# Score banks in a pool of their own, output sums in four one-bank tiles, and one store for each last result

## The chip, the cores and the metric

The kernel runs on one NeuronCore of a Trainium2 chip. The metric is device time in microseconds (us) for one launch. TensorE (PE in the profile) multiplies matrices; VectorE (DVE) and ScalarE (ACT) do elementwise work and are the only engines here that read PSUM, the accumulators' memory of eight banks of 128 x 512 float32; GpSimd (POOL) helps with splits of operands; SyncE (SP) issues nearly all DMAs. An engine runs its instructions in the order in which they were written for it, and waits on semaphores for the others.

## The reference

Attention with a threshold, then two MLPs in a row over the same 2304 tokens. All is float32.

```
scores = (q @ k^T) / 8                      # 4 batches, 8 heads, 576 x 576, head size 64
scores = where(scores >= max(scores) - tau, scores, -1e9)
attn   = softmax(scores);  y = attn @ v
x  = y, heads laid side by side              # 2304 x 512
h  = x @ w_in;   g = max(h, 0) + alpha * min(h, 0);   x = g @ w_out      # 512 -> 2048 -> 512
h  = x @ w2_in;  g = h - tanh(h);                     out = g @ w2_out   # 512 -> 2048 -> 512
```

## The kernel before

The tokens are cut into nine blocks of 256. Float32 operands are split into a high and a low part, and each product is three matmuls (high x high, low x high, high x low). Attention, the first MLP (blocks m = 0 to 8) and the second (m = 9 to 17) overlap. Each MLP block has eight pairs of steps over the 2048 hidden columns: `h_pair` or `twin_pair` computes h in the tiles `hp`, `pt` or `acc` (L915, L869), `split` makes g and its parts, `acc_pair` multiplies by the output weights and sums over the pairs.

All instructions are recorded with estimated costs and ranks, ordered once by the planner `Plan.order`, and then written out in that order with `run()`. The planner knows banks by keys of its own (`("c", 0)` to `("c", 3)` for the four output banks). The waits on semaphores are laid later, by the tile framework, and it keeps its books by tile: whoever touches a tile that another engine wrote or read waits for it, whichever columns it was.

PSUM is shared out at the start (L273 to L276). `sc` is two tiles of 1024 columns, so two banks each; `acc` two tiles of one bank; `hp` and `pt` one bank each. In attention a tile of `sc` holds the 576 scores of one head. Later its four banks hold output sums:

- In the last two blocks of the first MLP, which run as one ("wide"), `wide_products` (L1104) sums four column groups c = 0 to 3 into `acc[0]`, `acc[1]` and the two banks of `sc[1]`. At the end ScalarE copies c = 2, 3, 0, 1 out (`drain`, L1114), each is stored to DRAM and read back for the second MLP.
- In the second MLP `out_products` runs. Six of the eight pairs use Strassen's seven products (`emit_seven`, L1032) and two use plain ones (`emit_plain`, L1039). The quarter sums lie in half banks: numbers 1 and 6 in bank 0, 2 and 3 in bank 1, 7 and 5 in bank 2, 4 and 8 in bank 3. Banks 0 and 1 are the tile `sc[0]`, banks 2 and 3 `sc[1]`. A plain pair adds only to banks 1 and 3.
- After the eighth pair of a block ScalarE copies number 1 out of bank 0 (`p1`, L1062), VectorE adds numbers 6, 7, 5 and 5 to it in four operations of 128 x 256 (L1065), and then adds the whole banks 1 and 3 in two operations of 128 x 512 (`both`). Each of these two is followed by its store (`store`).

Rows of `out` go by batch, 576 each. Blocks 9 to 16 store 128 neighbouring rows with one DMA (L1085). Block 17 holds the last 64 rows of each of four batches, so its two results are stored as two pieces of 64 rows each (L1089), four DMAs in all.

Of the kernel before, what the change touches and what calls it, by code (L numbers as in the profile page):

```python
# [24 lines left out]
P = 128  # L25
# [53 lines left out]
class Plan:  # L79
# [9 lines left out]
    def add(self, engines, rank, emit, reads=(), writes=(), banks=(), takes=(), lag=0.0, after=(), late=False):  # L89

        n = len(self.ops)
        deps, order = set(), set(after)
        for k in reads:
            deps.update(self.written.get(k, ()))
        for k in writes:
            deps.update(self.written.get(k, ()))  # L100
            deps.update(self.read.get(k, ()))
        for k in reads:
            self.read.setdefault(k, []).append(n)
        for k in writes:
            self.written[k] = [n]
            self.read[k] = []
        for k in {k[:2] for k in (*reads, *writes)}:
            self.users.setdefault(k, []).append(n)
        for tag, _ in takes:
            if tag != "rw":  # L110
                if self.takers.get(tag, n) != n:
                    order.add(self.takers[tag])
                self.takers[tag] = n
        deps.discard(n)
        self.ops.append((engines, rank, emit, deps, order - deps, banks, takes, lag, "DVE" in engines and not banks and engines["DVE"] > 0.1, late))
        return n
# [119 lines left out]
def attention_mlp_mlp(ctx: ExitStack, tc: tile.TileContext, kv, q0, q1, tau, w1i, w1o, alpha, w2i, w2o, out):  # L236
# [33 lines left out]

    sc = [ppool.tile([P, 1024], F32, name=f"sc{k}") for k in range(2)]  # L273
    acc = [ppool.tile([P, 512], F32, name=f"acc{t}") for t in range(2)]
    hp = ppool.tile([P, 2, BLK], F32, name="hp")
    pt = ppool.tile([P, 4, P], F32, name="pt")  # L276

    hps = hp, pt.rearrange("p (k c) s -> p k (c s)", k=2)

# [9 lines left out]
    def take(pool, key, shape, dtype, tag, bufs):  # L289
        T[key] = pool.tile(shape, dtype, tag=tag, name=tag, bufs=bufs)  # L290
        return T[key]
# [716 lines left out]

    def half_bank(n):
        k = {1: 0, 6: 1, 2: 2, 3: 3, 7: 4, 5: 5, 4: 6, 8: 7}[n]  # L1010
        return sc[k // 4][:, k % 4 * BLK:(k % 4 + 1) * BLK], k // 2

    def two_banks(k):
        return sc[k // 2][:, k % 2 * 512:(k % 2 + 1) * 512]

    def out_products(p, rank):
        m, n = p // NPAIR, p % NPAIR
        w, g = ("wp", n), ("g", p)
        strassen = n in STRASSEN
        begins = n == out_order(m)[0]  # L1020

        seven = [(0, 0, 1), (2, 1, 2), (1, 6, 4), (3, 3, 5), (4, 4, 6), (5, 5, 7), (6, 2, 3)]
        begun_banks = set()

        def emit_seven(e, now):
            gh, gl = T[g], T["gl", p]
            wh, wl = T[w]
            for a, b, number in now:
                a, b = slice(a * P, (a + 1) * P), slice(b * BLK, (b + 1) * BLK)
                out_, bank = half_bank(number)  # L1030
                for i, (x, y) in enumerate(((gl, wh), (gh, wh), (gh, wl))):
                    e.matmul(out_, lhsT=x[:, a], rhs=y[:, b], start=(begins and i == 0 and number in (1, 2, 5, 4)),  # L1032
                             stop=(n == NPAIR - 1 and i == 2), skip_group_check=True)

        def emit_plain(e, k, t):
            wh, wl = (x[:, k * 512:(k + 1) * 512] for x in T[w])
            gh, gl = (T[g][:, part, k, t * P:(t + 1) * P] for part in range(2))
            for i, (x, y) in enumerate(((gl, wh), (gh, wh), (gh, wl))):
                e.matmul(two_banks(3 - 2 * t), lhsT=x, rhs=y, start=False, stop=(n == NPAIR - 1 and k == 1 and i == 2), skip_group_check=True)  # L1039

        if strassen:
            rows = [(*w, k, part) for k in range(4) for part in range(2)]
            for k, now in enumerate((seven[:1], seven[1:3], seven[3:5], seven[5:])):
                halves = {half_bank(x[2])[1] for x in now}
                add({"PE": 0.36 * len(now)}, rank + MLP_PE, lambda e, now=now: emit_seven(e, now), [*rows, (*g, 0), (*g, 1), ("gl", p, 0), ("gl", p, 1)],
                    [("c", x) for x in halves], [("c", x) for x in halves])
        else:
            for t in (1, 0):
                for k in range(2):
                    x = 3 - 2 * t  # L1050
                    add({"PE": 0.69}, rank + MLP_PE, lambda e, k=k, t=t: emit_plain(e, k, t), [(*w, k, 0), (*w, k, 1), (*g, 0), (*g, 1)], [("c", x)], [("c", x)])
        if n < NPAIR - 1:
            return
        o = [("o", 2 * m + t) for t in range(2)]

        def bank(number):
            return half_bank(number)[0]

        def p1(e):
            for k in range(2):  # L1060
                take(apool, o[k], [P, 512], F32, "o", BUFS["o"])
            copy(e, T[o[1]][:, :BLK], bank(1))  # L1062

        def total(e, out_, x, y):
            e.tensor_tensor(out=out_, in0=x, in1=y, op=ALU.add)  # L1065

        r = rank + MLP_G
        a, b = (lambda: T[o[1]][:, :BLK]), (lambda: T[o[1]][:, BLK:])
        c, d = (lambda: T[o[0]][:, :BLK]), (lambda: T[o[0]][:, BLK:])
        oa, ob, oc, od = [(*o[1], 0)], [(*o[1], 1)], [(*o[0], 0)], [(*o[0], 1)]  # L1070
        add({"ACT": 0.3}, r, p1, [("c", 0)], oa + [o[0], o[1]], [("c", 0)], takes=[("o", x) for x in o])
        add({"DVE": 0.35}, r, lambda e: total(e, b(), bank(6), a()), [("c", 0), *oa], ob, [("c", 0)])
        add({"DVE": 0.35}, r, lambda e: total(e, c(), bank(7), b()), [("c", 2), *ob], oc, [("c", 2)])
        add({"DVE": 0.35}, r, lambda e: total(e, d(), bank(5), c()), [("c", 2), *oc], od, [("c", 2)])
        add({"DVE": 0.35}, r, lambda e: total(e, b(), bank(5), b()), [("c", 2), *oc], ob, [("c", 2)])
        for t in (1, 0):
            x = 3 - 2 * t

            def both(e, t=t, x=x):
                total(e, T[o[t]], two_banks(x), T[o[t]])  # L1080

            def store(e, t=t):
                if m < 2 * NBLK - 1:
                    row = (m - NBLK) // 2 * S + (m - NBLK) % 2 * BLK + t * P
                    e.dma_start(out=out[row:row + P, :], in_=T[o[t]])  # L1085
                else:
                    for k in range(2):
                        row = (2 * t + k + 1) * S - D
                        e.dma_start(out=out[row:row + D, :], in_=T[o[t]][k * D:(k + 1) * D, :])  # L1089

            z = oa + ob if t else oc + od
            add({"DVE": 0.6}, r, both, [("c", x), *z], z, [("c", x)])
            add({"SYNC": 1.2}, r, store, z, [("out", m, t)], lag=3.0)

    def wide_products(p, rank):
        f = p - (NBLK - 2) * NPAIR
        banks = [acc[0], acc[1], two_banks(2), two_banks(3)]
        keys = [("acc", 0), ("acc", 1), ("c", 2), ("c", 3)]
        for c in range(4):
            def emit(e, c=c):  # L1100
                gh, gl = (T["g", p][:, part] for part in range(2))
                hi, lo = (weight(0, "o", part, f // 4)[:, f % 4, c * P:(c + 1) * P] for part in range(2))
                for n, (w, g) in enumerate(((hi, gh), (hi, gl), (lo, gh))):
                    e.matmul(banks[c], lhsT=w, rhs=g, start=(f == 0 and n == 0), stop=(f == NF - 1 and n == 2))  # L1104

            reads = [("w", (0, "o", f // 4), f % 4, part) for part in range(2)]
            add({"PE": 0.69}, rank + MLP_PE, emit, [*reads, ("g", p, 0), ("g", p, 1)], [keys[c]], [keys[c]])
        if f < NF - 1:
            return
        for c in (2, 3, 0, 1):  # L1110
            o = ("o", 2 * (NBLK - 2) + c)

            def drain(e, c=c, o=o):
                copy(e, take(apool, o, [P, 512], F32, "o", BUFS["o"]), banks[c])  # L1114

            def store(e, c=c, o=o):
                e.dma_start(out=wide_x1d[:, c], in_=T[o].rearrange("p (m s) -> p m s", m=2))

            add({"ACT": 0.478}, rank + MLP_G, drain, [keys[c]], [o], [keys[c]], takes=[("o", o)])
            add({"SYNC": 1.2}, rank + MLP_G, store, [o], [("x1d", m, c) for m in (NBLK - 2, NBLK - 1)], lag=3.0)  # L1120
# [199 lines left out]
```

## Time and profile before

| | us |
|---|---|
| median of 3 runs | 1054.56 (1054.54 to 1054.87) |
| the profiled execution: its time | 1052.59 |
| the profiled execution: its span in the trace | 1050.8 |
| TensorE busy (PE) | 1023.7 |
| VectorE busy (DVE) | 772.9 |
| ScalarE busy (ACT) | 618.4 |

The span is what the trace covers; the time of the same execution is 1.79 us longer, and the median of the runs another 1.97 us. Times in rows are from the start of the span. An end of a busy stretch of PE is modelled, and matmuls that follow one another overlap in the rows: a row of "x12" starts with its first matmul and ends with its last.

### The profile page before, as it was taken

To read this page: it belongs to the slowest core of one execution; us is meant where nothing else is said; L and a number is where in the kernel's file an instruction comes from. 1 tells how busy PE (TensorE), PEld (TensorE's weight loads), DVE (VectorE), ACT (ScalarE), POOL (GpSimd) and SP (SyncE) were. 2 spreads that over 40 slices of the span, in tenths; PEclk is the share of its full clock that TensorE was granted. 3 is DMA by queue.
4 is the path that set the end of the run, shared out by engine and by line. 5 is a ranking of instruction groups with operands and counts; after the bars stand their busy time and mean duration, and the time that the engine had idled before them with its cause. 6 is when DMAs were issued, how large, how long until landed. Compare 5 with 4: busy or idle time off the path is not lost.

```text
span 1050.8 us, 22486 instructions
## 1 busy us (share of the span) xinstructions
PE 1023.7 (97%) x8859; PEld 928.2 (88%) x8859; DVE 772.9 (74%) x1738; ACT 618.4 (59%) x1287; POOL 74.4 (7%) x101
## 2 busy tenths in 40 slices
PE   9979989999999999999999999999999999999997
PEld 7769879999999999998999888998898898899886
DVE  6998989878788778887857787674584484485465
ACT  6988888788788788887846554442312222331321
POOL 0122121001110111101100000000000000000000
PEclk9999999999999999999999999999999999999999
DMA  6678988758786557775585433200010010010000
GB/s 195 191 181 190 209 199 176 136 109 160 141 148 136 124 120 150 140 124 119 96 219 180 135 125 116 80 21 1 21 41 21 21 41 21 21 41 21 1 21 21
DMA packets 188890, 110.76 MB, mean 105 GB/s; under 512 B 158688, under 2 KB 171248, under 8 KB 188784
## 3 DMA queue, kind: packets, MB, share of 16 engines
q1 hardware_dynamic: 188480, 108.51, 44.8%
q8 instruction: 69, 1.13, 0.4%
q10 hardware_dynamic: 304, 0.82, 0.3%
q14 instruction: 37, 0.30, 0.1%
HBM read 61.58 MB, written 9.96 MB: 68 GB/s over the span
## 4 chain that ended last, share of the span: by engine, by line
PE 59%; DVE 2%; ACT 1%; DMA 1%; issue 1%; SPq 0%; DVEq 0%; ACTq 0%
PE sc L1032 13%; PE hp L915 10%; PE acc L869 6%; PE pt L915 5%; PE acc L1140 5%; PE sc L1039 5%; PE pt L869 3%; PE hp L869 3%; PE pt L679 2%; PE sc L1104 2%; PE acc L1104 2%; PE sc L700 1%; DVE st L573 1%; DMA eT<-rw 0%; ACT e L300 0%
## 5 line engine op out<-in xcount | busy, mean ns | idle before, releaser
L915 PE MATMUL hp<-x,i 128*128 128x256 f32 (+1 forms) x1584 | 230.9, 291 | 12.8 <-ACT e L300 5.6
L915 PEld LDWEIGHTS hp<-x,i 128*128 128x128 f32 x1584 | 206.1, 191 | 24.5 <-ACT e L300 6.1
L1140 PE MATMUL acc<-g,o 128*128 128x256 f32 x1232 | 165.7, 279 | 0.8 <-POOL g L303 0.8
L1140 PEld LDWEIGHTS acc<-g,o 128*128 128x128 f32 x1232 | 152.6, 188 | 4.4 <-POOL g L303 1.0
L300 ACT ACTIVATE e<-sc,st,qscale 128x576 f32<-128x576 f32 x144 | 118.0, 828 | 31.1 <-DVE st L576 18.9
L1032 PE MATMUL sc<-wp,g 128*128 128x256 f32 x756 | 135.8, 280 | 0.0
L1032 PEld LDWEIGHTS sc<-wp,g 128*128 128x128 f32 x756 | 115.8, 188 | 1.3
L618 DVE SCALAR_TENSOR_TENSOR rw<-e,st,rw 128x576 f16<-128x576 f32 x128 | 104.7, 835 | 10.3 <-ACT rw L295 9.7
L573 DVE TENSOR_REDUCE st<-sc 128x1 f32<-128x576 f32 x144 | 102.6, 750 | 13.1 <-PE sc L700 12.1
L583 ACT ACTIVATE e<-e,natau 128x576 f32<-128x576 f32 x144 | 110.9, 774 | 0.2
L1032 PE MATMUL sc<-wp,rw 128*128 128x256 f32 x378 | 106.1, 281 | 0.8 <-ACT o L295 0.8
L295 ACT ACTIVATE rw<-e,st 128x576 f16<-128x576 f32 x103 | 78.1, 771 | 18.3 <-DVE st L589 8.0
L295 ACT ACTIVATE g<-mr 128x512 fp32r<-128x512 f32 (+1 forms) x99 | 59.1, 597 | 47.8 <-PE sc L1104 16.7
L679 PE MATMUL pt<-eT,vs 128*64 128x256 f16 (+1 forms) x1584 | 73.3, 247 | 0.2 <-DMA eT<-rw 0.2
L1032 PEld LDWEIGHTS sc<-wp,rw 128*128 128x128 f32 x378 | 71.2, 188 | 2.3 <-ACT o L295 1.0
L303 DVE TENSOR_TENSOR g<-mr,g 128x512 fp32r<-128x512 f32 x80 | 55.6, 695 | 18.9 <-ACT g L295 18.4
L679 PEld LDWEIGHTS <-vs 128*64 128x64 bf16 x1584 | 65.0, 111 | 4.8 <-issue 0.4
L700 PE MATMUL sc<-kh,qh 64*128 64x320 f32 (+1 forms) x672 | 61.7, 310 | 4.4 <-ACT e L300 4.3
L869 PE MATMUL acc<-x,i 128*128 128x512 f32 x264 | 65.5, 395 | 0.0
L700 PEld LDWEIGHTS sc<-kh,qh 64*128 64x128 f32 x672 | 49.1, 185 | 13.2 <-ACT e L300 5.5
L869 PEld LDWEIGHTS acc<-x,i 128*128 128x128 f32 x264 | 48.9, 187 | 11.4
L915 PE MATMUL pt<-x,i 128*128 128x256 f32 (+1 forms) x352 | 58.0, 311 | 0.0
(246 smaller groups left out, 1707.4 us busy)
## 6 DMA issues: line engine op xcount, KB each, us to landing
vs<-in_kv_dram SPq DMA_DIRECT2D x58, 160.0 KB, 3.0
rw<-in_w1o_dram SPq DMA_DIRECT2D x16, 512.0 KB, 4.6
rw<-in_w2i_dram SPq DMA_DIRECT2D x16, 512.0 KB, 4.8
rw<-in_w2o_dram SPq DMA_DIRECT2D x16, 512.0 KB, 4.0
rw<-in_kv_dram SPq DMA_DIRECT2D x56, 144.0 KB, 3.0
rw<-in_w1i_dram SPq DMA_DIRECT2D x15, 512.0 KB, 4.8
out_dram<-o SPq DMA_DIRECT2D x16, 256.0 KB, 2.0
x1d<-o SPq DMA_DIRECT2D x14, 256.0 KB, 2.8
```

What stands on the lines that cost most here:

```text
L295: e.activation(out=out_, in_=in_, func=AF.Copy, **({} if scale is None else {"scale": scale}))
L300: e.activation(out=out_, in_=in_, func=AF.Prelu, alpha=alpha, **kw)
L303: e.tensor_tensor(out=out_, in0=in_, in1=hi.bitcast(F32), op=ALU.subtract)
L573: e.tensor_reduce(out=T[st][:, 0, j:j + 1], in_=x(s), axis=AX.X, op=ALU.max, negate=True)
L583: e.activation(out=w_, in_=w_, func=AF.Exp, bias=natau, scale=1.0, accum_out=T[st][:, 2, j:j + 1])
L618: e.scalar_tensor_tensor(out=x_[:, S + D:], in0=w_, scalar=r, in1=x_[:, :S], op0=ALU.mult, op1=ALU.subtract)
L679: e.matmul(po[HALVES[a]], lhsT=plane((k, a), part, c), rhs=eT(a, block), start=(i == 0), stop=(i == len(TERMS) - 1), skip_group_check=True)
L700: e.matmul(to(a, c), lhsT=x[HALVES[a], s], rhs=y[HALVES[a], c], start=(i == 0), stop=(i == len(terms) - 1))
L869: e.matmul(hq[k], lhsT=weight(1, "i", part, f // 4)[:, c, (f % 4) * P:(f % 4 + 1) * P], rhs=slots_of_x[x][:, :, c, :], start=(n0 + i == 0) ...
L915: e.matmul(hq if both_blocks else hq[:, k, :], lhsT=weight(l, "i", part, f // 4)[:, c, (f % 4) * P:(f % 4 + 1) * P], rhs=slots_of_x[x][:, ...
L1032: e.matmul(out_, lhsT=x[:, a], rhs=y[:, b], start=(begins and i == 0 and number in (1, 2, 5, 4)), stop=(n == NPAIR - 1 and i == 2), skip_g ...
L1140: e.matmul(acc[t][:, (c % 2) * BLK:(c % 2 + 1) * BLK], lhsT=w[:, c * P:(c + 1) * P], rhs=g[:, k, :], start=(f == 0 and n == 0 and c % 2 == ...
```

## The change

It does three things. The two `sc` tiles move from the general PSUM pool to a pool of their own, `spool`. That pool is released when the first output product is written out, and a new pool takes its four banks as four tiles `out0` to `out3` of one bank each; `two_banks` and `half_bank` hand these out, and `wide_products` fetches them only when it emits. And the last block stores each of its two results with one DMA, whose DRAM side is two pieces of 64 rows.

```
-    sc = [ppool.tile([P, 1024], F32, name=f"sc{k}") for k in range(2)]
     acc = [ppool.tile([P, 512], F32, name=f"acc{t}") for t in range(2)]
     hp = ppool.tile([P, 2, BLK], F32, name="hp")
     pt = ppool.tile([P, 4, P], F32, name="pt")
+    spool = tc.alloc_tile_pool(name="spool", bufs=1, space=PSUM)
+    sc = [spool.tile([P, 1024], F32, name=f"sc{k}") for k in range(2)]
+    banks_of_out = []
 
     hps = hp, pt.rearrange("p (k c) s -> p k (c s)", k=2)
 
...
 
     def half_bank(n):
         k = {1: 0, 6: 1, 2: 2, 3: 3, 7: 4, 5: 5, 4: 6, 8: 7}[n]
-        return sc[k // 4][:, k % 4 * BLK:(k % 4 + 1) * BLK], k // 2
+        return two_banks(k // 2)[:, k % 2 * BLK:(k % 2 + 1) * BLK], k // 2
 
     def two_banks(k):
-        return sc[k // 2][:, k % 2 * 512:(k % 2 + 1) * 512]
+        if not banks_of_out:
+            spool.release()
+            mpool = ctx.enter_context(tc.tile_pool(name="mpool", bufs=1, space=PSUM))
+            banks_of_out.extend(mpool.tile([P, 512], F32, name=f"out{n}") for n in range(4))
+        return banks_of_out[k]
 
     def out_products(p, rank):
         m, n = p // NPAIR, p % NPAIR
...
                     row = (m - NBLK) // 2 * S + (m - NBLK) % 2 * BLK + t * P
                     e.dma_start(out=out[row:row + P, :], in_=T[o[t]])
                 else:
-                    for k in range(2):
-                        row = (2 * t + k + 1) * S - D
-                        e.dma_start(out=out[row:row + D, :], in_=T[o[t]][k * D:(k + 1) * D, :])
+                    ends = out.rearrange("(b s) d -> b s d", s=S)[2 * t:2 * t + 2, S - D:, :]
+                    e.dma_start(out=ends, in_=T[o[t]])
 
             z = oa + ob if t else oc + od
             add({"DVE": 0.6}, r, both, [("c", x), *z], z, [("c", x)])
-            add({"SYNC": 1.2}, r, store, z, [("out", m, t)], lag=3.0)
+            add({"SYNC": 0.7}, r, store, z, [("out", m, t)], lag=3.0)
 
     def wide_products(p, rank):
         f = p - (NBLK - 2) * NPAIR
-        banks = [acc[0], acc[1], two_banks(2), two_banks(3)]
+        def home_of(c):
+            return acc[c] if c < 2 else two_banks(c)
+
         keys = [("acc", 0), ("acc", 1), ("c", 2), ("c", 3)]
         for c in range(4):
             def emit(e, c=c):
                 gh, gl = (T["g", p][:, part] for part in range(2))
                 hi, lo = (weight(0, "o", part, f // 4)[:, f % 4, c * P:(c + 1) * P] for part in range(2))
                 for n, (w, g) in enumerate(((hi, gh), (hi, gl), (lo, gh))):
-                    e.matmul(banks[c], lhsT=w, rhs=g, start=(f == 0 and n == 0), stop=(f == NF - 1 and n == 2))
+                    e.matmul(home_of(c), lhsT=w, rhs=g, start=(f == 0 and n == 0), stop=(f == NF - 1 and n == 2))
 
             reads = [("w", (0, "o", f // 4), f % 4, part) for part in range(2)]
             add({"PE": 0.69}, rank + MLP_PE, emit, [*reads, ("g", p, 0), ("g", p, 1)], [keys[c]], [keys[c]])
...
             o = ("o", 2 * (NBLK - 2) + c)
 
             def drain(e, c=c, o=o):
-                copy(e, take(apool, o, [P, 512], F32, "o", BUFS["o"]), banks[c])
+                copy(e, take(apool, o, [P, 512], F32, "o", BUFS["o"]), home_of(c))
 
             def store(e, c=c, o=o):
                 e.dma_start(out=wide_x1d[:, c], in_=T[o].rearrange("p (m s) -> p m s", m=2))
```

The order in which instructions stand on each engine does not move, apart from the stores; what moves are names and waits. In the rows below the number behind a tile's name tells tiles of one name apart (`sc0_89` is `sc[0]`, `out1_105` is `out1`), and in brackets stand the semaphores waited for: an engine's own counter, or one of the DMA's (DMAHW). Line numbers after are 2 to 7 higher (L1032 is L1038, L1039 is L1045, L1065 is L1071, L1089 is L1094).

ScalarE, at the end of the first MLP, where it copies out c = 2 and c = 3. Before:

```order
L927 ACTIVATE mr_9950<-pt_94 128x512 [waits DVE_49,PE_49]
L295 ACTIVATE o_9964<-sc1_90 128x512 [waits PE_49]
L295 ACTIVATE o_9972<-sc1_90 128x512
L295 ACTIVATE o_10012<-acc0_91 128x512 [waits DMAHW7_49,Activation_49]
L927 ACTIVATE mr_10024<-hp_93 128x512 [waits DVE_49,PE_49]
```

And in the changed kernel:

```order
L929 ACTIVATE mr_9961<-pt_92 128x512 [waits DVE_49,PE_49]
L297 ACTIVATE o_9975<-out2_106 128x512 [waits PE_49]
L297 ACTIVATE o_9983<-out3_107 128x512 [waits PE_49]
L297 ACTIVATE o_10023<-acc0_89 128x512 [waits DMAHW7_49,Activation_49]
L929 ACTIVATE mr_10035<-hp_91 128x512 [waits DVE_49,PE_49]
```

Before, the first copy waited for the last product of either column group, since both write `sc1`. Now each waits for the last product of its own group. The matmul that follows on TensorE and writes bank 2 waited for both copies; now it waits for the first, and one nine matmuls later, which writes bank 3, for the second.

TensorE, its last plain pair (t = 1 adds to bank 1, t = 0 to bank 3). Before:

```order
L1039 MATMUL sc0_89<-wp0_10255,g_13500 128x512 [waits DVE_49,Activation_49]
L1039 MATMUL sc0_89<-wp0_10255,g_13500 128x512
L1039 MATMUL sc0_89<-wp1_10256,g_13500 128x512
L1039 MATMUL sc0_89<-wp0_10255,g_13500 128x512 [waits DVE_49]
L1039 MATMUL sc0_89<-wp0_10255,g_13500 128x512
L1039 MATMUL sc0_89<-wp1_10256,g_13500 128x512
L1039 MATMUL sc1_90<-wp0_10255,g_13500 128x512 [waits DVE_49]
L1039 MATMUL sc1_90<-wp0_10255,g_13500 128x512
L1039 MATMUL sc1_90<-wp1_10256,g_13500 128x512
L1039 MATMUL sc1_90<-wp0_10255,g_13500 128x512 x2
L1039 MATMUL sc1_90<-wp1_10256,g_13500 128x512
```

And in the changed kernel:

```order
L1045 MATMUL out1_105<-wp0_10266,g_13511 128x512 [waits DVE_49]
L1045 MATMUL out1_105<-wp0_10266,g_13511 128x512
L1045 MATMUL out1_105<-wp1_10267,g_13511 128x512
L1045 MATMUL out1_105<-wp0_10266,g_13511 128x512 x2
L1045 MATMUL out1_105<-wp1_10267,g_13511 128x512
L1045 MATMUL out3_107<-wp0_10266,g_13511 128x512 x2
L1045 MATMUL out3_107<-wp1_10267,g_13511 128x512
L1045 MATMUL out3_107<-wp0_10266,g_13511 128x512 x2
L1045 MATMUL out3_107<-wp1_10267,g_13511 128x512
```

Before, the three waits are for the copy of number 1, the first add and the fourth add, which all read the other bank of the same tile. Now the one wait left is for g, the operand. On the other side ScalarE's copy now waits for the last product into bank 0, VectorE's first add for that copy alone, and its second for the last product into bank 2.

SyncE, the last stores. Before:

```order
L1085 DMA out_0_dram<-o_12743 128x512 [waits DMAHW7_49,DVE_49]
L1085 DMA out_0_dram<-o_13239 128x512 [waits DMAHW0_49,DVE_49,Activation_49]
L1085 DMA out_0_dram<-o_13238 128x512 [waits DMAHW1_49,DVE_49]
L1089 DMA out_0_dram<-o_13522 64x512 [waits DVE_49,Activation_49]
L1089 DMA out_0_dram<-o_13522 64x512 [waits DMAHW3_49]
L1089 DMA out_0_dram<-o_13521 64x512 [waits DMAHW4_49,DVE_49]
L1089 DMA out_0_dram<-o_13521 64x512 [waits DMAHW5_49]
```

And in the changed kernel:

```order
L822 DMA rw_12578<-wide_x1d_79 128x4x256 [waits DMAHW5_49,DMAHW2_49,DVE_49]
L1091 DMA out_0_dram<-o_13250 128x512 [waits DMAHW0_49,DVE_49,Activation_49]
L1091 DMA out_0_dram<-o_13249 128x512 [waits DMAHW1_49,DVE_49]
L1094 DMA out_0_dram<-o_13533 2x64x512 [waits DVE_49,Activation_49]
L1094 DMA out_0_dram<-o_13532 2x64x512 [waits DMAHW3_49,DVE_49]
```

Four stores of 64 rows have become two whose DRAM side counts 2, then 64, then 512; the side in SBUF counts 128 partitions, as in the other stores.

## Rows read from the trace of the kernel before

**Rows 1.** The page's head and the engines' busy time over the span.

```profile
span 1050.8 us, 22486 instructions
...
PE 1023.7 (97%) x8859; PEld 928.2 (88%) x8859; DVE 772.9 (74%) x1738; ACT 618.4 (59%) x1287; POOL 74.4 (7%) x101
```

**Rows 2.** TensorE's waits, 600 to 1051 us: total, times, longest.

```profile
PE sc L1039 <- DVE o L1065: 0.9, 2, 0.6
PE sc L1032 <- ACT o L295: 0.8, 1, 0.8
PE sc L1039 <- ACT o L295: 0.5, 1, 0.5
```

**Rows 3.** Timeline, end of the first MLP: start, duration, work, [idle before].

```profile
661.31 0.39 PE L1104 MATMUL sc<-g,o3b 128*128 128x512 f32 x1
...
662.01 0.40 PE L1104 MATMUL sc<-g,o3b 128*128 128x512 f32 x1
662.25 0.28 PE L1032 MATMUL sc<-wp,rw 128*128 128x256 f32 x1
...
662.44 1.09 ACT L295 ACTIVATE o<-sc 128x512 f32<-128x512 f32 x2 [2.20 <-PE sc L1104]
...
663.58 0.38 PE L1032 MATMUL sc<-wp,rw 128*128 128x256 f32 x1 [0.83 <-ACT o L295]
```

**Rows 4.** Timeline, TensorE going from Strassen to plain products without a wait.

```profile
1030.70 0.40 PE L1032 MATMUL sc<-wp,g 128*128 128x256 f32 x2
...
1030.94 2.92 PE L1039 MATMUL sc<-wp,g 128*128 128x512 f32 x12
```

**Rows 5.** Timeline, the last 11 us.

```profile
1040.18 0.40 PE L1032 MATMUL sc<-wp,g 128*128 128x256 f32 x2
...
1040.88 0.40 PE L1032 MATMUL sc<-wp,g 128*128 128x256 f32 x2
1041.32 0.39 ACT L295 ACTIVATE o<-sc 128x256 f32<-128x256 f32 x1 [4.36 <-PE sc L1032]
...
1042.81 2.47 DVE L1065 TENSOR_TENSOR o<-sc,o 128x256 f32<-128x256 f32 x5 [2.81 <-PE sc L1039]
...
1044.54 1.66 PE L1039 MATMUL sc<-wp,g 128*128 128x512 f32 x6 [0.29 <-DVE o L1065]
1045.35 2.70 SPq L1089 DMA_DIRECT2D out_dram<-o  x4
1046.23 0.69 DVE L1065 TENSOR_TENSOR o<-sc,o 128x512 f32<-128x512 f32 x1 [0.96 <-PE sc L1039]
```

**Rows 6.** Chain of waits, the third and fourth add of the last block.

```profile
1043.72 0.77 DVE o L1065 x2
```

**Rows 7.** Timeline of SyncE's queue, the third and fourth of the last stores.

```profile
1046.95 1.10 SPq L1089 DMA_DIRECT2D out_dram<-o  x2
```

**Rows 8.** Line 1089, stores of 64 rows: ns min/median/max of an issue; landing.

```profile
L1089 SPq DMA_DIRECT2D out_dram<-o x4: 466/565/587, 1045.4 to 1047.5; - x4
...
DMA to landing us min/median/max: 2.2/2.3/2.4
```

**Rows 9.** Line 1085, stores of 128 rows, the same columns.

```profile
L1085 SPq DMA_DIRECT2D out_dram<-o x16: 332/333/348, 702.7 to 1022.2; - x16
...
DMA to landing us min/median/max: 2.0/2.0/4.1
```

**Rows 10.** DMA view, 1045.3 to 1050 us in 40 slices: busy tenths, packets, queue.

```profile
DMA  0000000000469968897983046996779896200000
...
DMA packets 320, 0.52 MB, mean 112 GB/s; under 512 B 64, under 2 KB 64, under 8 KB 320
...
q1 hardware_dynamic: 320, 0.52, 48.2%
```

**Rows 11.** DMA view, 1020.1 to 1024.6 us, two stores of line 1085.

```profile
DMA packets 289, 0.53 MB, mean 118 GB/s; under 512 B 32, under 2 KB 32, under 8 KB 288
...
q1 hardware_dynamic: 288, 0.52, 30.6%
```

More of the change, by code (lines that the diff above doesn't have):

```diff
@@ L276, in attention_mlp_mlp @@
     pt = ppool.tile([P, 4, P], F32, name="pt")
+    spool = tc.alloc_tile_pool(name="spool", bufs=1, space=PSUM)
+    sc = [spool.tile([P, 1024], F32, name=f"sc{k}") for k in range(2)]
+    banks_of_out = []
     hps = hp, pt.rearrange("p (k c) s -> p k (c s)", k=2)
@@ L1010, in half_bank @@
         k = {1: 0, 6: 1, 2: 2, 3: 3, 7: 4, 5: 5, 4: 6, 8: 7}[n]
-        return sc[k // 4][:, k % 4 * BLK:(k % 4 + 1) * BLK], k // 2
+        return two_banks(k // 2)[:, k % 2 * BLK:(k % 2 + 1) * BLK], k // 2
     def two_banks(k):
-        return sc[k // 2][:, k % 2 * 512:(k % 2 + 1) * 512]
+        if not banks_of_out:
+            spool.release()
+            mpool = ctx.enter_context(tc.tile_pool(name="mpool", bufs=1, space=PSUM))
+            banks_of_out.extend(mpool.tile([P, 512], F32, name=f"out{n}") for n in range(4))
+        return banks_of_out[k]
     def out_products(p, rank):
@@ L1086, in store, with home_of @@
                 else:
-                    for k in range(2):
-                        row = (2 * t + k + 1) * S - D
-                        e.dma_start(out=out[row:row + D, :], in_=T[o[t]][k * D:(k + 1) * D, :])
+                    ends = out.rearrange("(b s) d -> b s d", s=S)[2 * t:2 * t + 2, S - D:, :]
+                    e.dma_start(out=ends, in_=T[o[t]])
             z = oa + ob if t else oc + od
             add({"DVE": 0.6}, r, both, [("c", x), *z], z, [("c", x)])
-            add({"SYNC": 1.2}, r, store, z, [("out", m, t)], lag=3.0)
+            add({"SYNC": 0.7}, r, store, z, [("out", m, t)], lag=3.0)
     def wide_products(p, rank):
         f = p - (NBLK - 2) * NPAIR
-        banks = [acc[0], acc[1], two_banks(2), two_banks(3)]
+        def home_of(c):
+            return acc[c] if c < 2 else two_banks(c)
         keys = [("acc", 0), ("acc", 1), ("c", 2), ("c", 3)]
@@ L1103, in emit @@
                 for n, (w, g) in enumerate(((hi, gh), (hi, gl), (lo, gh))):
-                    e.matmul(banks[c], lhsT=w, rhs=g, start=(f == 0 and n == 0), stop=(f == NF - 1 and n == 2))
+                    e.matmul(home_of(c), lhsT=w, rhs=g, start=(f == 0 and n == 0), stop=(f == NF - 1 and n == 2))
             reads = [("w", (0, "o", f // 4), f % 4, part) for part in range(2)]
@@ L1113, in drain @@
             def drain(e, c=c, o=o):
-                copy(e, take(apool, o, [P, 512], F32, "o", BUFS["o"]), banks[c])
+                copy(e, take(apool, o, [P, 512], F32, "o", BUFS["o"]), home_of(c))
             def store(e, c=c, o=o):
```

1 line of the change is left out of this document (removed).

## The prediction

> **What bounds the kernel now.** I read the page's head first: TensorE is busy 1023.7 of 1050.8 us, so other engines matter only where TensorE waits or where nothing follows it [rows 1]. The view of TensorE's waits from 600 us on shows how rare that is: four waits in all, 0.8 us for ScalarE at one place and 0.9 and 0.5 us at another [rows 2]. The timeline puts the first at 663 us, between the two MLPs [rows 3], the other three behind 1041 us, in the last pair [rows 5]. So no wait of TensorE that the change removes in the blocks between is worth anything: there TensorE is never late, and VectorE's and ScalarE's adds lie beside its next block. Worth something are the change of MLPs and the tail, and in the tail also the stores, since nothing lies beside them.
>
> **Between the MLPs.** ScalarE copies out c = 2 and then c = 3 in 1.09 us, from 662.44 on, 0.03 us after the last product of c = 3 (662.01 + 0.40). It had been idle for 2.20 us. TensorE does three matmuls of line 1032 from 662.25 and resumes only at 663.58 [rows 3]. With a tile for each bank the first copy waits for the products of c = 2 alone, which end at 661.31 + 0.39 = 661.70: it runs from 661.73 to about 662.33. TensorE would go on after three matmuls of 0.12 us each (two take from 1030.70 to 1030.94 [rows 4]), at 662.61, and finds bank 2 free. The second copy ends at about 663.0, and bank 3 is wanted nine matmuls later, at 663.69. The gain is 663.58 - 662.61 = 0.97 us. It is kept: what follows is paced by TensorE without a wait up to 1041 us [rows 2], and the work of VectorE, ScalarE and the loads there is set off by it, so it comes earlier too. What is late next is nothing.
>
> **A wait that is added.** The first product into a new tile waits for the last score product, 583 instructions earlier on TensorE itself. It is long done; I cost it at nothing, and were it to drain the array once, it would be one matmul, 0.4 us [rows 3]. Waits that only move, at the beginnings of blocks, are for work that TensorE waited for before too.
>
> **The last pair.** Before, matmuls and adds take turns, since banks 0 and 1 are one tile. TensorE's last Strassen pair of matmuls starts at 1040.88 [rows 5]; without a wait the twelve plain ones start 0.24 us later and take 2.92 us [rows 4]: 1041.12 to 1044.04. They need only g, which was ready before them. Bank 0 has its last product two triples before the end, at 1040.18 + 0.40 = 1040.58. ScalarE's copy then takes 0.39 us, to about 1041.0, and the four adds, which take 1043.72 + 0.77 - 1042.81 = 1.68 us [rows 5, 6], end at 1042.7. The fifth, on bank 1, whose six matmuls end near 1042.7 as well (five steps of 0.23 us, and the last one's 0.39 us), ends 0.79 us later as it did before (1042.81 + 2.47 - 1044.49), at 1043.51 instead of 1045.28. The sixth follows the last matmul, 1044.06 + 0.69 = 1044.75, instead of 1046.92. So the two results are there 1.77 and 2.17 us earlier, and 0.97 us more with the gain above: 1042.54 and 1043.78.
>
> **The stores.** Before, the four issues take 2.70 us from 1045.35; the third starts at 1046.95 and the fourth, 1.10 - 0.57 us later, at 1047.48 [rows 5, 7, 8]. The span ends 3.32 us after that. The strip of DMA activity shows data from slice 10, 1046.48, which is 1.13 us after the first issue, to the end of slice 34, 1049.41, which is 1.39 us before the end of the span [rows 1, 10]. Two of four issues of 0.57 us go. What the new form of store costs no row shows, so I bound it by the number of DMA engines that share it:
>
> - Sixteen. Then it is a store of 128 rows like line 1085's, landing in 2.0 us [rows 9], plus 0.24 us for the slower issue (565 against 332 ns [rows 8, 9]): 2.24 us, against 2.3 before. The span would end 3.26 us after the second issue at 1043.81, at 1047.07: 3.73 us earlier.
> - Two. The DRAM side of the new form counts 2 outermost. If engines are dealt whole outermost pieces, 64 rows fall to each of two engines. A packet of one row, 2048 bytes, holds an engine for 86 ns where 128 partitions are stored (30.6% of 16 engines for 4.5 us, over 256 packets [rows 11]) and 142 ns in the tail, where 64 are (48.2% for 4.7 us [rows 10]). Both stores go the same way, one behind the other: 128 packets x 86 ns = 11.01 us on each of the two. The first is issued 0.07 us after its add, at 1042.61, and data begins 1.13 us later, at 1043.74; the last ends at 1054.75, and 1.39 us more make 1056.14: 5.34 us later than before. At 142 ns it would be 18.2 us, and 12.5 us later; if an engine had two packets in hand at a time, 5.5 us, and 0.2 us earlier than before.
>
> Which one? Every DMA of the kernel before has an outermost count of 16, 64, 128 or 512 on both sides, and the view counts 64 closing packets under 512 bytes for the four stores of the tail and 32 for two stores of line 1085: sixteen each [rows 10, 11]. That fits dealing by outermost pieces, and it would fit dealing by single rows. But the first explains sixteen closings for all these lists from one number of each list, and a list that counts 2 is the first that has fewer pieces than engines. I take two engines, at the 86 ns of the store that also spans 128 partitions, since the two halves of SBUF are then read by one engine each. The Trainium skill's page "DMA: Bandwidth & Descriptors" says it outright, in "Why a DMA increments its semaphore by 16 and not by 1": the number of engines is the largest one up to 16 that divides the slowest counts of both sides, and only these engines close the transfer. By that rule it is 2 for counts of 128 and 2; the sixteen closings seen agree with it, and no row here shows a smaller number. The same page's 27 GiB/s for an engine would make an estimated 71 ns of a packet, and 3.4 us later in place of 5.34.
>
> **Sum.** In the profiled execution 0.97 us is gained between the MLPs, 1.77 us at the first of the last two results, and the stores then take 13.53 us (1.13 + 11.01 + 1.39) from the first issue to the end in place of 5.45: 8.08 lost, 2.74 gained, 5.34 us later. Its span becomes 1056.1 us and its time 1052.59 + 5.3 = 1057.9; the runs' median stands 1.97 us above this execution, so 1054.56 + 5.3 = 1059.9 us.
>
> **Rivals.**
> - The stores spread over sixteen engines (the other side). Then all three parts gain, and 3.73 us less make 1050.8 us. For it: sixteen closings for every DMA so far. Against: none of these lists has fewer than sixteen outermost pieces. It decides from four shared engines on: 256 packets x 86 ns over four are 5.5 us, 5.5 less than over two, and 5.34 were lost.
> - Two engines for a store, but others for the second. Its data runs from 1043.81 + 1.13 = 1044.94 for 64 x 86 ns = 5.5 us, and the end is at 1051.83: 1.03 us later, 1055.6 us. For it: nothing ties the two stores to one pair. Against: one queue issues both, with the same list.
> - The waits don't go, since the framework still ties the new tiles together, and two engines store. Then the first issue stays at 1045.35, the end comes at 1045.35 + 13.53 = 1058.88, 8.1 us later, 1062.6 us. Against: the waits have left the instructions.
>
> **Chances.** Two shared engines 0.75, sixteen 0.15, two pairs of engines 0.07, the waits stay 0.03. A difference of 0.2% (2.1 us) is what a measurement of this kernel can tell from none. Slower by more: the first and the last, 0.78; faster by more: sixteen, 0.15; within: two pairs, 0.07. The likeliest case alone runs from 1057.5 us (near the faster packet) to 1067 us (packets of 142 ns). For 8 in 10 the range takes in the two pairs as well and leaves out sixteen: 1055 to 1067 us.
>
> **What will show it.** In the profile after: no wait of TensorE at all near 663 us and in the last pair, and the plain twelve in one run of 2.9 us; the fifth add ending some 2.7 us earlier than before; two stores with 2 closing packets each in place of 16, a DMA strip in the tail that stays at one tenth (2 of 16 engines) for about 11 us, and a landing of the second store of some 11 us. Sixteen closings, a strip at 9 and a landing of 2.3 us would prove me wrong, and the time would be near 1051 us.

## The result, and the profile after

The changed kernel takes 1061.72 us, the median of 4 runs (1060.82 to 1062.88). Beside it on the same chip the kernel before takes 1054.59 us (4 runs, 1054.54 to 1054.87). The ratio is 1.0064, with a 95% interval of [1.0049, 1.0079]: slower by 5.2 to 8.3 us. 1059.9 us and 5.34 us more were forecast, by way of two DMA engines for both stores. One run each of the fifth and the sixth experiment below took some 2550 us; the ratios leave these two out, and without them the medians are 1055.14 and 1050.53 us.

The profiled execution of the changed kernel took 1061.06 us. The head of its page answers to [rows 1]:

```profile
span 1059.3 us, 22489 instructions
...
PE 1024.9 (97%) x8859; PEld 929.4 (88%) x8859; DVE 773.1 (73%) x1738; ACT 618.6 (58%) x1287; POOL 75.6 (7%) x101
```

The work of each engine is within 1.2 us of what it was, and the span is 8.5 us longer. So nearly all of the difference is time in which TensorE computes nothing. The view of TensorE's waits from 600 us to the end is empty: the four waits of [rows 2] are gone.

The timeline at the end of the first MLP (start, duration, work, [idle before]) answers to [rows 3]:

```profile
663.78 0.39 PE L1111 MATMUL out<-g,o3b 128*128 128x512 f32 x1
...
664.21 1.30 ACT L297 ACTIVATE o<-out 128x512 f32<-128x512 f32 x2 [1.50 <-PE out L1111]
664.47 0.40 PE L1111 MATMUL out<-g,o3b 128*128 128x512 f32 x1
664.71 0.28 PE L1038 MATMUL out<-wp,rw 128*128 128x256 f32 x1
664.83 0.39 PE L1038 MATMUL out<-wp,g 128*128 128x256 f32 x2
665.05 0.28 PE L1038 MATMUL out<-wp,rw 128*128 128x256 f32 x1
```

ScalarE copies c = 2 out at 664.21, behind the last product of c = 2 (663.78 + 0.39) and while TensorE still works on c = 3. The rows of line 1038 follow without the hole of 0.83 us.

The last pair, to be read against [rows 5]:

```profile
1041.99 0.39 ACT L297 ACTIVATE o<-out 128x256 f32<-128x256 f32 x1 [3.65 <-PE out L1038]
...
1042.26 0.40 PE L1038 MATMUL out<-wp,g 128*128 128x256 f32 x2
1042.41 2.53 DVE L1071 TENSOR_TENSOR o<-out,o 128x256 f32<-128x256 f32 x5 [1.03 <-ACT o L297]
1042.50 2.92 PE L1045 MATMUL out<-wp,g 128*128 128x512 f32 x12
1045.01 1.71 SPq L1094 DMA_DIRECT2D out_dram<-o  x2
1045.45 0.69 DVE L1071 TENSOR_TENSOR o<-out,o 128x512 f32<-128x512 f32 x1 [0.52 <-PE out L1045]
```

The twelve plain matmuls are one run of 2.92 us. The five adds now lie beside them, and the last one follows the last matmul. Then comes what was lost: both stores are issued by 1046.7 (1045.01 + 1.71), and the span runs on to 1059.3.

The DMA view of 1042 to 1059.3 us in 40 slices (busy tenths of 16 engines, packets, the queue's share) answers to [rows 10]:

```profile
DMA  0000000000110110111111111111111111110000
...
DMA packets 260, 0.52 MB, mean 30 GB/s; under 512 B 4, under 2 KB 4, under 8 KB 260
...
q1 hardware_dynamic: 260, 0.52, 8.7%
```

The same 0.52 MB are stored, but with 4 closing packets (under 512 B) for two stores, where four stores had 64. The strip stays at one tenth, which is 2 of 16 engines, for some 12 us; before, it mostly stood at 4 to 9. The share gives a packet's price: 8.7% of 16 engines for 17.3 us is 24.1 us over 256 packets, 94 ns.

Where the 8.5 us of span are, with times taken from one instruction to another so that a shift of the whole drops out:

- Between the MLPs: from the last product of c = 2 to the last Strassen pair 1042.26 - 663.78 = 378.48 us, before 1040.88 - 661.31 = 379.57 [rows 3, 5]: 1.09 us gained.
- The first store's issue comes 1045.01 - 1042.26 = 2.75 us behind that pair, before 1045.35 - 1040.88 = 4.47 [rows 5]: 1.72 gained.
- From the first issue to the end 1059.3 - 1045.01 = 14.29 us, before 5.45: 8.84 lost.
- That makes 6.03. The other 2.47 us (663.78 against 661.31) were there before any instruction that the change touches; the third experiment is about them.

### The profile page after: what moved, and what is told of

It reads as the page before. It is cut to its first block, busy times and chain, and to the rows that moved or that the text cites. A ratio compares the mean times of both kernels' runs of the same rounds, so it can differ in the third digit from the quotient of the medians.

```text
span 1059.3 us, 22489 instructions
## 1 busy us (share of the span) xinstructions
PE 1024.9 (97%) x8859; PEld 929.4 (88%) x8859; DVE 773.1 (73%) x1738; ACT 618.6 (58%) x1287; POOL 75.6 (7%) x101
## 3 DMA queue, kind: packets, MB, share of 16 engines
q8 instruction: 69, 1.13, 0.5%
## 5 line engine op out<-in xcount | busy, mean ns | idle before, releaser
L917 PE MATMUL hp<-x,i 128*128 128x256 f32 (+1 forms) x1584 | 231.5, 291 | 11.6 <-ACT e L302 5.3
L1038 PE MATMUL out<-wp,g 128*128 128x256 f32 x756 | 135.8, 280 | 0.0
L1038 PEld LDWEIGHTS out<-wp,g 128*128 128x128 f32 x756 | 115.8, 188 | 1.3
L1038 PE MATMUL out<-wp,rw 128*128 128x256 f32 x378 | 106.0, 280 | 0.0
L1038 PEld LDWEIGHTS out<-wp,rw 128*128 128x128 f32 x378 | 71.3, 188 | 1.3
```

Of the source, the lines that this page charges most:

```text
L917: e.matmul(hq if both_blocks else hq[:, k, :], lhsT=weight(l, "i", part, f // 4)[:, c, (f % 4) * P:(f % 4 + 1) * P], rhs=slots_of_x[x][:, ...
```

## The experiments

Theory A is that of the prediction: both merged stores go to the same two DMA engines, since their outermost count in DRAM is 2, and a tile of two banks is what ties TensorE to the copies and adds. Its rivals are said in each expectation. The last column is the time from the first issue of the last stores to the end of the span, in each one's profiled execution. The experiments ran on three chips (1 to 4, 5 to 8, and 9), with the kernel before beside them on each, at medians of 1053.5 to 1053.8 us. A ratio is to the kernel before on the same chip.

| kernel | time, us | ratio to before, 95% | closings | issue to end, us |
|---|---|---|---|---|
| before | | | 64 | 5.45 |
| changed | 1061.72 | 1.0064 [1.0049, 1.0079] | 4 | 14.29 |
| 1 stores only | 1062.33 | 1.0083 [1.0071, 1.0095] | 4 | 14.23 |
| 2 pools only | 1050.16 | 0.9965 [0.9955, 0.9976] | 64 | 5.18 |
| 3 banks moved | 1054.48 | 1.0007 [0.9994, 1.0021] | 64 | 5.49 |
| 4 pools, two queues | 1051.06 | 0.9972 [0.9961, 0.9983] | 64 | 4.91 |
| 5 four pieces | 1055.37 | 1.0019 [1.0009, 1.0029] | 8 | 9.79 |
| 6 sixty-four pieces | 1050.72 | 0.9973 [0.9960, 0.9986] | 32 | 4.63 |
| 7 interleaved | 1049.66 | 0.9967 [0.9954, 0.9979] | 32 | 4.62 |
| 8 merged, two queues | 1060.89 | 1.0065 [1.0047, 1.0084] | 4 | 14.23 |
| 9 wide tiles | 1054.14 | 0.9998 [0.9985, 1.0012] | 64 | 5.46 |

**1. The stores alone.** The kernel before, with the new stores.

```diff
-                    for k in range(2):
-                        row = (2 * t + k + 1) * S - D
-                        e.dma_start(out=out[row:row + D, :], in_=T[o[t]][k * D:(k + 1) * D, :])
+                    ends = out.rearrange("(b s) d -> b s d", s=S)[2 * t:2 * t + 2, S - D:, :]
+                    e.dma_start(out=ends, in_=T[o[t]])
```

> The kernel before, with only the last stores changed: one DMA for each of the two last results, its DRAM side counting 2, 64, 512. Theory A (each such store runs on two DMA engines, both stores on the same two): the first issue stays near 1045.35 us of the kernel before, and from it to the end the changed kernel took 14.27 us (1045.01 to 1059.28), so the span ends near 1059.6, 8.8 us later: 1063.4 us; 4 closing packets for the two stores; the plain twelve of TensorE still interrupted by three waits. Rival B (the changed kernel lost its time elsewhere, the stores cost little): at most 1056 us. On the later start of the tail in the changed kernel (it ran 2.46 us behind at 655 us, before any of the changed stores): if it comes from the place of the score banks in PSUM (theory P), this kernel has none of it at 655 us; if such shifts come and go from run to run (theory R), it can have some too.

Its waits, TensorE from 600 us on (total, times, longest), are those of [rows 2]:

```profile
PE sc L1039 <- DVE o L1065: 0.9, 2, 0.6
PE sc L1032 <- ACT o L295: 0.8, 1, 0.8
PE sc L1039 <- ACT o L295: 0.5, 1, 0.5
```

And its DMA view, 1044.9 to 1060.9 us:

```profile
DMA  0000000011011011111111111111111111110000
...
DMA packets 260, 0.52 MB, mean 33 GB/s; under 512 B 4, under 2 KB 4, under 8 KB 260
...
q1 hardware_dynamic: 260, 0.52, 9.4%
```

9.4% of 16 engines for 16 us is 94 ns per packet again. The merged stores alone cost 0.8%, 8.8 us, and from the first issue to the end it is 8.78 us more than before (14.23 against 5.45).

**2. The pools alone.** The changed kernel, with the four old stores (the edit above, undone).

> The changed kernel with the four last stores of the kernel before. Theory A: the loss is gone and the two gains are left, 1.08 us between the MLPs and 2.16 us in the last pair, 3.2 us: 1051.4 us if the attention stage runs as in the kernel before (theory R on average, with a spread of some 2 us between runs), 1053.8 us in every run if the place of the score banks costs 2.46 us there (theory P). Rival B: no better than 1059 us. Sixteen closing packets for each of the four stores.

Without a wait of TensorE from 600 us on, it takes 1050.16 us: 3.7 us less than before [2.5 to 4.7]. The last add and the stores of its profile:

```profile
1044.02 2.46 SPq L1095 DMA_DIRECT2D out_dram<-o  x4
1044.47 0.69 DVE L1071 TENSOR_TENSOR o<-out,o 128x512 f32<-128x512 f32 x1 [0.52 <-PE out L1045]
```

This version beats both kernels. The change was a gain and a loss put together: 0.9965 x 1.0083 = 1.0048, just below the interval of the changed kernel, which was timed apart from these two (1.0049 to 1.0079); with the intervals of the two factors it is 1.0026 to 1.0071.

**3. The banks' place.** The 2.47 us that were lost ahead of the change could come from the score tiles now lying in other banks, or from scatter between executions. The kernel before, with only these tiles allocated later:

```diff
-    sc = [ppool.tile([P, 1024], F32, name=f"sc{k}") for k in range(2)]
     acc = [ppool.tile([P, 512], F32, name=f"acc{t}") for t in range(2)]
     hp = ppool.tile([P, 2, BLK], F32, name="hp")
     pt = ppool.tile([P, 4, P], F32, name="pt")
+    sc = [ppool.tile([P, 1024], F32, name=f"sc{k}") for k in range(2)]
```

> The kernel before with one edit: the two score tiles are taken from the same pool after the other accumulators, so that they lie in banks 4 to 7 and acc, hp and pt in banks 0 to 3, as in the changed kernel; tiles, waits and stores as before. Theory P (the place costs time in attention): 1.5 to 2.5 us more, 1056 to 1057 us in every run. Theory R (shifts come and go, whatever the banks): the median within 0.5 us of the kernel before, or a spread of some 2 us without a side.

The ratio is 1.0007 [0.9994, 1.0021]. No cost of the place shows, but this interval alone reaches 2.2 us and does not shut out all of theory P. The ninth experiment does: its score tiles lie as in the changed kernel, its last stores are the old ones, its waits are those of the kernel before, and its ratio is at most 1.0012, or 1.3 us. What there is instead is scatter: the kernel before itself ran between 1051.1 and 1056.0 us on this chip in 24 runs, between 1050.6 and 1059.3 us beside the ninth experiment in 17, and the profiled execution of this experiment took 1059.67. The two rows below are the last product of c = 2 and the last add of that execution:

```profile
668.36 0.39 PE L1104 MATMUL sc<-g,o3b 128*128 128x512 f32 x1
...
1053.31 0.69 DVE L1065 TENSOR_TENSOR o<-sc,o 128x512 f32<-128x512 f32 x1 [0.97 <-PE sc L1039]
```

They stand 7.05 and 7.08 us behind [rows 3, 5]: nearly all of it arose before 668 us, and stays the same afterwards. The first experiment, whose banks lie as before, stood 1.32 us behind at the same product (662.63 us). So 2.47 us in one execution of the changed kernel are within what unchanged work shows. Matched matmul by matmul in the two traces, the changed kernel is 0.12 us ahead where the kernel before stands at 150 us, 0.18 us behind at 250, 1.53 at 320 and 2.47 at 655. The largest step shows in the table by stretch, 250 to 320 us (length, busy time of TensorE, its weight loads, VectorE, ScalarE and GpSimd, granted clock, DMA share, GB/s), before and then changed:

```profile
250.00:320.00 70.00, 68.43 (x774) 64.66 (x774) 57.11 (x125) 58.07 (x127) 11.13 (x15) 1.00 0.79 153
```

```profile
250.00:320.00 70.00, 67.65 (x762) 63.44 (x761) 56.01 (x121) 56.97 (x125) 10.35 (x14) 1.00 0.78 148
```

762 matmuls were done instead of 774, at a granted clock of 1.00, the higher of the two levels (2.4 GHz), in both. It is 1.00 in both from 150 to 655 us on the whole, so the clock is not what made these 2.47 us. What did was not found.

**4. Four stores from two queues.** The pools, with the second store of each result issued by ScalarE.

```diff
-                    ends = out.rearrange("(b s) d -> b s d", s=S)[2 * t:2 * t + 2, S - D:, :]
-                    e.dma_start(out=ends, in_=T[o[t]])
+                    for k in range(2):
+                        row = (2 * t + k + 1) * S - D
+                        (nc.scalar if k else e).dma_start(out=out[row:row + D, :], in_=T[o[t]][k * D:(k + 1) * D, :])
```

> The changed kernel with the last results stored as before in two pieces of 64 rows, but the second piece of each issued from ScalarE's queue in place of SyncE's, so that the two issues of 0.57 us lie beside each other. Theory A: as the kernel with four stores from one queue, less about 0.5 us: 1050.9 us by theory R, 1053.3 us by theory P; each store closes with 16 packets. Rival: ScalarE's issue starts later than SyncE's second one would (over 0.57 us after the add), and nothing is gained against four stores from one queue.

The end comes 4.91 us after the first issue, 0.27 us sooner than with one queue and not the 0.5 expected. The rival, a late start of ScalarE's issues, is not the reason: the two queues begin 0.03 us apart (1043.29 and 1043.32 us). In time it can't be told from the second experiment.

**5. Four pieces.** The test of the rule itself: the same bytes and partitions, and a count of 4 in place of 2.

```diff
-                    ends = out.rearrange("(b s) d -> b s d", s=S)[2 * t:2 * t + 2, S - D:, :]
+                    ends = out.rearrange("(b s) d -> b s d", s=S)[:, S - D + t * D // 2:S - D + (t + 1) * D // 2, :]
```

> The changed kernel, with the 128 rows of each last store cut as four pieces of 32 rows in place of two of 64, by their place in the result: its counts there are 4, 32 and 512. (The last 256 rows land in other places than the reference has them; bytes, packets and work are the same.) Theory A, the outermost count in DRAM sets how many DMA engines carry a store: four engines, so 8 closings for the two stores, a DMA share of some 2 tenths while they run, 256 x 94 ns / 4 = 6.0 us of data, and from the first issue to the end 1.2 + 6.0 + 1.2 = 8.4 us in place of the 14.3 of the changed kernel: a time some 5.9 us below it and some 3.2 us above the pools alone with four stores. Theory B, a store of both partition halves by one DMA always goes to two engines: 14.3 us from issue to end, the time of the changed kernel. Theory C, what is slow is the merging itself and not the count of engines (a packet of such a store takes longer wherever it runs): the closings show other than 8, or the packets other than about 94 ns.

Its DMA view, 1043 to 1053.8 us:

```profile
DMA  0000000014132012312222222222222211000000
...
DMA packets 264, 0.52 MB, mean 49 GB/s; under 512 B 8, under 2 KB 8, under 8 KB 264
```

Four closings for each store, and two tenths, which fits 4 of 16 engines: theory A, not B. The size was off: 9.79 us from issue to end instead of 8.4. The strip shows why. Its steady part begins late. From 1045.28, where data begins, to 1047.2 only 26 packets started; in the 4 us after that it was 190 (the same view, of 1045 to 1047.2 and of 1047.2 to 1051.2 us):

```profile
DMA packets 26, 0.05 MB, mean 24 GB/s; under 512 B 0, under 2 KB 0, under 8 KB 26
...
q1 hardware_dynamic: 26, 0.05, 21.1%
...
DMA packets 190, 0.38 MB, mean 95 GB/s; under 512 B 4, under 2 KB 4, under 8 KB 190
...
q1 hardware_dynamic: 190, 0.38, 25.6%
```

At the later pace 26 packets take 0.55 us, so the slow start costs 1.4 us. The engines are busy in it, with packets that take longer: 21.1% of 16 engines for 2.2 us over 26 packets is 286 ns for each, where it is 86 ns later (25.6% for 4 us over 190). Over the whole store a row took 107 ns (15.9% for 10.8 us over 256). So the second sign of theory C, packets other than 94 ns, did come, through the first packets; the next two experiments decide against theory C.

**6 and 7. A count of 64.** The seventh changes the store's list alone; in the sixth the tokens are laid out for it when the block's input is split.

```diff
-                    e.dma_start(out=ends, in_=T[o[t]])
+                    e.dma_start(out=ends.rearrange("k s d -> s k d"), in_=T[o[t]])
```

The sixth has this as well, with `hi` and `lo` reading and writing through the two views:

```diff
         def x():
-            return T[raw].bitcast(F32).rearrange("p (c s) -> p c s", c=4)
+            y = T[raw].bitcast(F32).rearrange("p (c s) -> p c s", c=4)
+            return y if m >= NBLK else y.rearrange("p c (t k s) -> p (c t) s k", t=2, k=2)
+
+        def to(part):
+            y = x_part(part, m)
+            return y if m >= NBLK else y.rearrange("p c (t s k) -> p (c t) s k", t=2, k=2)
```

> The changed kernel, one DMA for each last result, but with the tokens of the last narrow block laid out in another order when its input is split in high and low parts, so that a store's counts in DRAM are 64, 2 and 512; the result is the same. Theory A (the outermost count in DRAM sets the engines): 16 engines, 16 closings for each store, from the first issue to the end 4.6 to 5.2 us as with four stores, and a time within 0.5 us of the pools alone with four stores, unless the reordered reads of the split cost something in the MLP. Theory B (two engines for any such merged store): 14.3 us from issue to end.

> The changed kernel, only with the store's counts in DRAM in the order 64, 2 and 512, without any reordering ahead of it (the last 256 rows land in other places than the reference has them). As the run before, without what the reordered split may cost: theory A 16 engines and 4.6 to 5.2 us from the first issue to the end; theory B 14.3 us.

The stores of the sixth, its timeline and then its DMA view of 1044.8 to 1050.4 us:

```profile
1045.77 1.73 SPq L1099 DMA_DIRECT2D out_dram<-o  x2
1046.22 0.69 DVE L1076 TENSOR_TENSOR o<-out,o 128x512 f32<-128x512 f32 x1 [0.53 <-PE out L1050]
```

```profile
DMA  0000000000000000899981008999810000000000
...
DMA packets 288, 0.52 MB, mean 94 GB/s; under 512 B 32, under 2 KB 32, under 8 KB 288
...
q1 hardware_dynamic: 288, 0.52, 24.3%
```

Sixteen closings for each store, eight to nine tenths, and 4.63 us from issue to end. A store by one DMA isn't slow in itself; the order of the counts in its list made it so. A packet holds an engine for 85 ns here (24.3% of 16 engines for 5.6 us over 256). The rearranged split costs nothing that can be told: the two ratios lie within each other's intervals, and with the second experiment's. So merging on sixteen engines gains about half a microsecond from issue to end over four stores, and nothing that these times resolve.

**8. Merged stores from two queues.**

```diff
-                    e.dma_start(out=ends, in_=T[o[t]])
+                    (nc.scalar if t else e).dma_start(out=ends, in_=T[o[t]])
```

> The changed kernel, with the second of its two merged stores issued from ScalarE's queue instead of SyncE's. Theory A2, a store with the outermost count 2 takes the same two engines from whichever queue: data of both stores on one pair, 256 packets of 94 ns over two engines, 12.0 us, from the first issue to the end 13.5 to 14.3 us, the time of the changed kernel less at most 0.6. Theory D, each queue has a pair of its own: 64 packets of 94 ns on each of four engines, 6.0 us of data, 8 us from issue to end, some 6 us faster than the changed kernel.

Its timeline of the two issues, then the DMA view of 1043.5 to 1059.5 us:

```profile
1045.27 1.14 ACTq L1094 DMA_DIRECT2D out_dram<-o  x1
...
1046.43 0.66 SPq L1094 DMA_DIRECT2D out_dram<-o  x1
```

```profile
DMA  0000000010110111111111111111111111110000
...
q10 hardware_dynamic: 130, 0.26, 5.1%
q1 hardware_dynamic: 130, 0.26, 4.2%
```

Both queues are at work, and the strip still never goes above one tenth. 14.23 us from issue to end fit two engines for both, and not four (8 us). From 1053 to 1054 us both stores are on their way, and each queue moves 12 packets (the DMA view of that stretch):

```profile
q1 hardware_dynamic: 12, 0.02, 6.3%
q10 hardware_dynamic: 12, 0.02, 6.3%
```

A queue that is alone moves twice as many: 24 from 1050 to 1051 us (q10, where q1 has 2) and 26 from 1056 to 1057 (q1). With a pair of engines for each queue neither would halve the other. No record names an engine; that it is the same pair follows from this, the share and the time.

**9. Two tiles of two banks.** Which of the two edits of the pools removes the waits? The pools as in the second experiment, with the old width of the tiles:

```diff
-            banks_of_out.extend(mpool.tile([P, 512], F32, name=f"out{n}") for n in range(4))
+            outs = [mpool.tile([P, 1024], F32, name=f"out{n}") for n in range(2)]
+            banks_of_out.extend(outs[n // 2][:, n % 2 * 512:(n % 2 + 1) * 512] for n in range(4))
```

> The pools alone with the four old stores, but the pool that follows the attention's holds the second MLP's outputs in two tiles of two banks in place of four tiles of one. Theory A, the gain on TensorE comes from one tile for each bank, since a tile of two banks ties both banks' work together: the waits of the kernel before come back (0.8 us at the end of the first MLP, 0.9 and 0.5 us in the last pair), the last add starts 6.0 us after the last Strassen pair of matmuls in place of 3.9, and the time is that of the kernel before, within 0.1%, 3 to 4 us above the pools alone. Theory B, the gain comes from the release of the score banks (their place, or a tie of the outputs to the scores' tiles): no wait of TensorE near 660 us, the add at 3.9 us, and a ratio of about 0.997 to the kernel before.

(The 6.0 and 3.9 us in it run to the end of the last add, not to its start.) Its waits, from 600 us on:

```profile
PE out L1046 <- DVE o L1072: 0.9, 2, 0.6
PE out L1039 <- ACT o L297: 0.8, 1, 0.8
PE out L1046 <- ACT o L297: 0.5, 1, 0.5
```

The same four waits with the same sizes, under the new pool's name, 6.03 us from the last Strassen pair to the end of the last add, and a ratio of 0.9998. Releasing the score banks gave nothing by itself; it made room for four tiles, and these gave the whole gain.

## Why the prediction was right, and where its sizes were off

- **What bounds the kernel.** Only the change of MLPs and the tail were said to be worth anything. Outside these the two traces differ by the 2.47 us from the attention and by nothing else.
- **Between the MLPs.** 0.97 us predicted, 1.09 measured. The waits left, and nothing else became late; the ninth experiment shows that the tile's width was the cause.
- **The added wait,** costed at nothing: the first product into a new tile starts at 579.2 us (`out2`, L1111), and the view of TensorE's waits over the whole span has no line for L1111, L1038 or L1045.
- **The last pair.** 1.77 and 2.17 us predicted for the two results, 1.72 (to the first issue) and 2.16 (to the end of the last add: 3.88 us behind the last Strassen pair, before 6.04) measured.
- **The stores on two engines,** on which everything hung. The forecast chose between two readings that [rows 10, 11] could not tell apart, since every list in the kernel before counts 16 or more outermost. 4 closings, one tenth, and the row of 2, 4 and 64 pieces with 14.29, 9.79 and 4.62 us settle it. By the rule of the Trainium skill's page "DMA: Bandwidth & Descriptors", in "Why a DMA increments its semaphore by 16 and not by 1", the closings of a store are 2, 4 and 16 for the lists tried, and the traces agree at all three.
- **The term that was mis-sized.** 13.53 us from the first issue to the end were predicted (1.13 + 11.01 + 1.39), 14.29 came: 1.2 us until data begins at 1046.2, 11.6 us of data, and 1.5 us from 1057.8 to the end. The packet's price was nearly right: in the steady part, 1049.4 to 1057.4 us, 201 packets start, 199 of them rows, so one in 80 ns on each of two engines; by the share, as the 86 were worked out, a row took 84 ns (13.1% of 16 engines for 8 us). What the sum lacked is a slow start. From 1046.2 to 1049.4 it is 48 packets (the DMA view of the changed kernel, 1046.2 to 1049.4 and 1049.4 to 1057.4 us):

```profile
DMA packets 48, 0.10 MB, mean 31 GB/s; under 512 B 0, under 2 KB 0, under 8 KB 48
...
q1 hardware_dynamic: 48, 0.10, 12.8%
...
DMA packets 201, 0.41 MB, mean 51 GB/s; under 512 B 2, under 2 KB 2, under 8 KB 201
...
q1 hardware_dynamic: 201, 0.41, 13.1%
```

  At the later pace these take 1.9 us instead of 3.2, so 1.3 us were lost; the mean of 94 ns hides this. The two engines are busy all the while (12.8% of 16 is 2.05), with 137 ns for each packet. In the trace's records 14 of these 48 took 142 to 393 ns, and every row behind them at most 84. That 11.01 came so near to 11.6 is in part luck: 128 rows at 80 ns are 10.2, and the slow start made up for the rest.
- **The sum.** 5.34 us later predicted, 6.03 in the traces without the scatter, and 5.2 to 8.3 by the runs. The forecast of 1059.9 us is 1.8 us short of the measured median: 0.7 from the sum's terms, the rest no larger than the scatter that the third experiment showed.
- **The rivals.** Sixteen engines is what the sixth and seventh experiments have, by another list: ratios of 0.9973 and 0.9967, where 1050.8 over 1054.56, that is 0.9964, was worked out for that rival. In that rival's price the prediction put the turning point at four engines, 5.5 us of data, where nothing would be lost. That was wrong: the fifth experiment, on four, takes 9.79 us from issue to end where 1.13 + 5.5 + 1.39 make 8.0, and it is slower than before (1.0019 [1.0009, 1.0029]) in spite of the gains on TensorE. Two pairs of engines fell with the changed kernel's strip and with the eighth. Waits that stay fell with the empty view; the ninth shows what it would have taken.

What stays open: why the first packets of a store on few engines are so slow (it showed on two and on four, at some 15 and 14 packets in a us, so four began no faster than two; on sixteen, in the sixth and seventh experiments, no row took more than 91 ns); what counts other than 2, 4 and 64, or a small count on the SBUF side, do; and what scatters in the attention.

## What to carry to other kernels

Before several DMAs are merged into one, look at the outermost count of the new list in DRAM: lists that begin with 2 put 0.52 MB on two engines and cost 8.8 us, where the same bytes in lists that begin with 64 took 4.6 us in all. Where producer and consumer take turns in PSUM, give each bank a tile of its own: the gain here was the tile's width, and not the pool or the banks' place. And a change with two independent parts is to be timed in parts: this one hid a version that was 3.7 us faster than before behind a store that cost 8.8.

## What the runs showed of the hardware beyond that

- A row of 2048 bytes held an engine for 142 ns where stores of 64 partitions ran on sixteen engines [rows 10], for 117 ns where two queues issued the two halves beside each other (fourth experiment, 30.2% of 16 engines for 6.2 us), for 85 ns in merged stores of 128 partitions on sixteen, and for 84 ns in the steady part of the stores on two. The merged stores on two engines had the cheaper packets, and that did not help them.
- Two queues did not bring more engines for the merged stores (14.23 us from issue to end on two queues, 14.29 on one), and hardly a shorter end for the four old ones (4.91 against 5.18 us).
- Unchanged work in the attention scattered by up to 7 us between executions of kernels whose work there is the same, more than any gain this change could have had.
